# A new order table for all engines of a recurrence and gating kernel, and the shift of a normalisation made only where it is read

## The chip, the cores and the metric

The kernel runs on one core of a Trainium2 chip. A core has a matrix engine (TensorE, PE in the profile), a vector engine (VectorE, DVE), a scalar engine (ScalarE, ACT), a general engine (GpSimd, POOL) and a sync engine (SyncE, SP) that here only issues transfers. Each works through its own queue of instructions in order, and semaphores hold an instruction back until what it needs is there. The metric is device time in microseconds (us) of one execution. Of the kernel before, three executions gave a median of 138.45 us (138.4 to 139.81).

## The reference

Two stages follow each other. The first is a gated linear recurrence over 4 batches, 8 heads, 768 steps, heads of 48; the second mixes its output over the sequence and gates it.

```
# stage 1, per batch and head
for t in range(768):
    state = alpha[t][:, None] * state + outer(k[t], v[t])      # 48 x 48
    y[t] = q[t] @ state
x = y with heads side by side                                    # 4 x 768 x 384
# stage 2
h = relu(x @ w_in);  u, v = h[..., :512], h[..., 512:]
v_n = (v - mean(v)) / sqrt(var(v) + 1e-6)                        # over the 512
v_s = w_spatial @ v_n + b_spatial                                # 768 x 768, over the sequence
out = (u * v_s) @ w_out                                          # 4 x 768 x 384
```

## The kernel before, in words

The sequence is cut into chunks of 128 steps, six to a batch, 24 in all. Inside a chunk the recurrence becomes matrix products: logarithms of alpha are summed by products with triangles of ones (`half`, `cum`, `cums`), exponentials of the sums scale k and q (`einv`, `eexp` on ScalarE; `kt`, `qt` as products), scaled k and q are transposed (`tr`, `trk`) and copied out of PSUM (`ev`, `evs`), their product is masked (`sc`, then `m` or `ms` on VectorE), and the masked product times v plus q times the old state gives y (`y`, `ya`), copied to SBUF as xT (`xe`). `upd`, `z`, `S`, `sb` carry the state from chunk to chunk; `vb` and `vp` bring v into place. The first four chunks are done together (`four_chunks`, pair numbers 0 and 1), chunks 4 and 5 as a pair (`pair`, number 2), chunks 6 to 9 together again (3 and 4), and the rest one by one (`single`).

Stage 2 works on tiles of 128 rows. `v` projects a tile to the 512 columns that are normalised, `ve` applies relu; `bn` (two VectorE instructions, lines 1068 and 1069) takes mean and variance; `rs` (ScalarE, lines 1078 and 1079) takes the reciprocal root for two tiles at once; `nm` (VectorE, line 1085, two instructions for a pair of tiles) writes shift = -mean * rstd; `vn` normalises a tile, on VectorE as (v - mean) * rstd (line 1097) or on ScalarE as v * rstd + shift (line 1093). Only ScalarE's form reads the shift. `u` and `ue` make the other half. `s` mixes over the sequence with the turned spatial weights (tiles 0 to 3 of a batch in a first part, tiles 4 and 5 in a second), `se` adds the bias on VectorE (line 1153), `g` multiplies by u (mostly GpSimd, line 190), `o` projects out, `oe` copies out of PSUM, `st` stores. The weights come as fp32 through two buffers, are cast to bf16 (`cast`), and the spatial ones are transposed on TensorE (`wt`, line 1018) and copied (`we`). A third load of weights needs the casts of the first to be done, a fourth those of the second, and so on.

Each of these is an entry of a list `ops`, made in the order of the program text, with the entries it depends on and the engines that may do it. The order in which all engines get their work is not computed in the kernel: it is written out in the string `PLAN` (lines 42 to 88). A word such as `P62@0:512#0` says: entry 62, on PE, its result in PSUM bank 0, and ahead of it a dummy product of 512 columns into bank 0. `D`, `A`, `G`, `S` stand for VectorE, ScalarE, GpSimd and SyncE. `replay` (line 110) goes through the words and emits each entry. As every engine works in order, the table fixes, for each engine, what it does and after what; waits between engines are put in from the data. The dummy products keep TensorE busy where the table expects it to have nothing to do.

Helpers hide some lines: copies are recorded at lines 179 and 181, relu at 185 and 187, products of two tensors at 190, and all accumulating matrix products of stage 2 at 1006.

Of the kernel before, what the change touches and what calls it, by code (L numbers as in the profile page):

```python
# [47 lines left out]
P123@7,3 P141@2 S20 G276 G277 G278 G17 G19 G18 D124 D125 P151@6 P187@7,4 P126@3 S23 S274 S273 D185 A152 A127 G186 G183
G113 G114 D182 P190@5,6 A189 A192 A142 P144@3 D137 P139@4 D188 D191 A140 G22 G21 D153 D143 P199@6,5 P196@2,7 P162@4
A280 A145 P287@0 A163 P154@1 P160@3 A279 A288 A155 D200 D201 D198 D197 D164 P193@4 A161 P156@7 A157 A165 D194 D146  # L50
P158@5 A159 G195 P202@1,2 P203 S26 A204 A147 D166 P290@4 P37@5,7 D38 P34@3,6 G24 S275 S384 S396 G25 S503 S29 D35
P207@1 D148 D208 D36 A39 A289 P205 P281@7 P40@3,5 A206 A282 A167 G10 D42 P210@2 D149 D150 D41 S385 S386 D168 D209 S398
S397 P284@5 P223@6 P219@3 P221@1 A211 A291 A224 A285 D212 A283 A220 A213 D295 D301 A286 A292 D214 D222 D215 A216
P225@6 P233@2 P217@3 P229@7 P237@0 A218 A28 D298 G297 G27 D304 G294 P226 D227 G300 G303 P43@3,5 D45 P230 P234 D231
D235 A293 A44 P46@4,6 P306@5,1 D308 P238 P49@7,3 D50 D51 A48 A47 A307 P309@2,6 P315@1,4 P312@5,7 P249@3 P250 A310 A316
A314 A296 A311 A299 D313 D317 D239 G236 D251 P338@4,1 P332@7,5 P245@0 P246 G302 G305 D333 D339 G232 P318@7,6,3,2 G240
G228 D340 D319 A507 G33 D334 D321 D247 P253@4 P330@7,1 P254 P241@5 P242 G320 A388 A400 A30 A337 A331 A32 G322 P389@0
D255 P345@7,6 D243 D324 D347 A390 P341@4 A391 P335@5 G31 G325 D394 D327 D346 G393 P401@3 A342 A336 A402 A403 P257@1
A392 S492 S387 A258 P259@4 P356@2 S399 G404 G248 G323 G326 S491 S557 P343@0,7 D405 P351@3,5 P407@1,6 A357 D328 A344
A350 A408 D353 D352 P359@2 G252 G395 P348@7 A349 P354@3 D409 S505 S494 S506 P418@6,1 P413@5,0 D358 S493 S504 S559 S547  # L60
S545 S608 S558 S548 S546 A355 A360 D415 D420 P508@7 P366@3 P410@0 P371@2 P377@1 D411 D414 A260 A509 P375@0 D419 A495
D361 A372 A561 P262@5 P496@6 G244 G329 G406 G256 A367 A376 A510 D368 G412 A497 A498 P416@0 P421@3 A422 G514 G502 G500
D378 D379 D513 G512 A417 P264@2 P267@4 A499 A362 A380 A268 D363 D501 P426@0 P423@1 P435@3 P437@6 D381 A365 A427 A424
P433@4 A434 A438 A382 D263 D436 P269@0 D364 D265 D425 D428 D383 P518@1 P369@4 A511 A270 P562@6 P373@2 A374 A429 A549
P439@7 A565 P526@0 D440 D519 P453@3 D430 D431 A432 A563 A564 D370 P449@7 P550@1 P515@2,5 A516 A551 A553 D517 A552 P454
D455 D527 D567 G566 G520 G554 G456 P441@4 P442 P445@5 D443 P450 D451 P465@6 P446 D555 D447 P530@7,4 P521@2,0 P569@1,3
D522 G448 G452 P469@5 P466 P457@2 P470 D523 D531 D532 G528 G444 D471 S620 A556 P572@7 D573 A570 P458 S622 S609 S560
A612 D467 D459 P613@4 P524@5 P533@1 A624 S610 A571 P576@7,3 P585@6,0 G574 A614 A525 D586 A615 A534 P625@5 A626 A568
G472 P535@2 A627 P461@1 S621 S611 S727 S715 S718 S623 S717 G617 D618 D578 D577 S730 S729 P473@6 G628 G575 P538@3
P581@7 A536 A616 A539 P462 S781 S716 A474 D629 P631@5,4 D587 A633 D463 D582 S728 A719 P588@3 S783 S769 S782 S770 S832  # L70
S771 A589 S784 S772 G619 G529 P579@1 A580 D632 D537 P634@7 P479@6 A630 A480 P720@5 G583 G468 D635 G636 A721 P642@3,4
P637@0,2 D540 G460 G584 P476@7 P601@6 P593@1 D643 D639 D638 A731 A723 D644 G726 G464 A602 A738 G724 P590@3 P597@6 A591
P732@0 D603 D592 A735 D477 P645@4 P640@3 A541 D542 D543 D594 A646 P485@2 A641 A785 A598 A486 D544 P650@4 P657@7 P742@6
A651 D743 D652 A733 A604 D605 D607 P488@3 P661@4 A658 A662 A734 P647@6 A489 A773 G736 P595@1 D648 D606 P482@4 D649
A483 A722 D744 P663@7 A664 D737 P599@6 P659@4 P786@3 A653 A600 P673@7 P669@0 P750@6 A596 A787 A788 P774@1 A775 A789
A776 S481 S844 S833 S834 A836 A780 S835 S845 A660 S846 D654 D655 D656 D751 D725 P674 P670 P677@6 P685@5 D671 P678
P665@0 D791 D752 D675 D779 G778 G792 D679 P796@7 P666 G790 D797 P686 G672 D687 D667 P739@6,4 P793@7,3 A848 A777 D794
P693@5 A740 A795 G680 G676 P805@0 P694 P849@7 P837@6 A838 A839 A850 A840 A851 D741 P745@3,4 P754@1,2 D695 G798 G668
D746 D806 D755 P689@5 P690 D691 D747 P681@3 P700@0 P682 P697@5 G843 D756 A698 D683 P703@4 D853 D842 D704 A701 P757@5
A758 P748@0 A749 A799 P800@6,7 D802 G841 G852 P809@3,2 P855@4,5 G807 G684 G696 G688 A856 G692 D810 P759@0 S847 P858@7  # L80
P762@3 D811 D801 P709@2 P812@6 A753 A760 P803@0 A857 D859 D761 D854 A813 A804 A763 P861@5,7 P866@4,1 S699 P712@6 D863
D868 D764 D867 D862 P825@7 A826 D827 P821@1 P817@3 P814@7 A818 A765 A815 A822 G860 P869@4 A870 S702 A713 S478 S266
S484 S490 S487 S705 S261 S475 S271 G808 P864@5 D816 P823@3 P819@1 D865 P874@4 D766 D768 A824 S714 A828 A820 A875 A767
A710 D829 P871@3 D830 D831 P887@5 P885@1 P881@4 D876 D872 D873 A877 D878 D879 P913@6 P706@2 A707 P893@3 P883@7 P897@0
A884 A886 A882 A888 P889@2 D880 P894 D895 G896 P890 P898 P905@5 P906 D891 D899 P901@2 P902 G900 P914 P909@0 P910
P917@3 D903 D892 D915 G916 D904 P926@6 P920@2 P918 S708 A927 S928 A921 S922 S711 D911 D907 D908 P923@6 G912 D919
P929@2 A930 D924 S925 S931 P935@3 D936 S937 P932@6 A933 S934 P938@3 D939 S940
"""

PAIRS = (2,)
QUADS = (0,3)
PLAIN = (0, 2)
IDLE = 16
STORE_TWO = (0, 2, 4)

# [1178 lines left out]
```

## Time and profile before

| | |
|---|---|
| median of three executions | 138.45 us |
| profiled execution | 139.19 us, of which the profile's span is 137.4 us |
| PE, DVE, ACT, POOL busy | 131.0, 120.8, 108.0, 87.2 us |
| read from memory, written | 23.60 MB, 4.72 MB |
| TensorE clock granted | 1.0 throughout |

The span runs from the first to the last instruction; some 1.8 us of the profiled execution lie around it. Busy time is a mean over the whole span, and the kernel has stages with different limits: it begins with loads (DMA queues are nearly full for the first 38 us, a mean of 313 GB/s), then the batches follow each other through all engines, and the last 14 us hold only the last batch's mixing, output projection and stores. In a row of the timeline the columns are start, length, engine, line, operation, output and inputs, shapes, count, and in brackets the engine's idle time before it with what ended it. A merged row with x2 or x4 holds instructions that follow each other; each is a little longer than its distance to the next, since the next one starts before the first has written out.

### The profile page before, as it was taken

The page shows a single profiled execution, that of the slowest core. Times are in us where ns is not written, and L with a number is a line of the kernel's source. Part 1 is how long each engine was busy: PE and PEld are TensorE (multiplying, and loading weights), DVE is VectorE, ACT ScalarE, POOL GpSimd, SP SyncE. Part 2 cuts the span into 40 slices and gives each one's busy share as a digit, 9 for nine tenths or more (in the row PEclk, how much of TensorE's full clock was granted, in tenths as well). Part 3 has the DMA queues.
Part 4 walks back from the last instruction along what each step waited for, and adds up shares of the span by engine and source line. Part 5 has one row for each costly group of instructions (what it writes and reads, how often), then busy time and mean ns, then how long its engine had stood idle before and what let it go on. Part 6 is the DMA issues. An engine that isn't in the chain of part 4 may idle for free.

```text
span 137.4 us, 5308 instructions
## 1 busy us (share of the span) xinstructions
PE 131.0 (95%) x2122; PEld 79.2 (58%) x2122; DVE 120.8 (88%) x300; ACT 108.0 (79%) x261; POOL 87.2 (63%) x146
## 2 busy tenths in 40 slices
PE   6899998999999999999999999999999999999990
PEld 3365554564646566566657666656566765565560
DVE  6259999979999999999899999997999999974871
ACT  3476998899989889999997989999965796954041
POOL 7365899967399789972079989620799842003560
PEclk9999999999999999999999999999999999999999
DMA  3999999599989796899999797899991497101055
GB/s 83 371 371 382 341 321 347 132 374 383 366 164 261 159 218 127 163 184 192 195 190 209 143 205 147 167 194 226 190 181 23 158 390 257 66 0 57 0 203 203
DMA packets 76473, 28.66 MB, mean 209 GB/s; under 512 B 63008, under 2 KB 74912, under 8 KB 76448
## 3 DMA queue, kind: packets, MB, share of 16 engines
q1 hardware_dynamic: 76416, 28.32, 78.6%
q8 instruction: 16, 0.26, 0.8%
q14 instruction: 9, 0.07, 0.2%
q0 software_dynamic: 32, 0.00, 0.0%
HBM read 23.60 MB, written 4.72 MB: 206 GB/s over the span
## 4 chain that ended last, share of the span: by engine, by line
PE 76%; ACT 6%; DVE 6%; DMA 5%; issue 3%; POOL 2%; SPq 0%; POOLq 0%; ACTq 0%
PE bank L1006 53%; DMA kc<-in_k_dram 5%; PE bank L961 3%; PE bank L945 3%; PE bank L989 3%; PE bank L417 2%; PE bank L855 2%; PE bank L899 2%; PE bank L837 2%; PE bank L933 2%; DVE vn L1097 1%; PE bank L795 1%; PE bank L772 1%; ACT uT L185 1%; DVE w_spT L181 1%
## 5 line engine op out<-in xcount | busy, mean ns | idle before, releaser
L1006 PE MATMUL bank<-w_spT,vn 128*128 128x384 bf16 x192 | 35.8, 327 | 0.3 <-DVE vn L1097 0.3
L190 POOL TENSOR_TENSOR gT<-vs,uT 128x384 bf16<-128x384 f32 x28 | 25.7, 933 | 14.3 <-DVE vs L1153 14.1
L190 POOL TENSOR_TENSOR kt<-kc,binv 128x384 bf16<-128x384 f32 x22 | 20.3, 931 | 20.3 <-ACT binv L909 15.2
L1006 PEld LDWEIGHTS <-vn 128*128 128x128 bf16 x192 | 17.4, 98 | 11.7 <-DVE vn L1097 0.7
L1006 PE MATMUL bank<-w_in,xT 128*128 128x512 bf16 x72 | 19.1, 380 | 0.2 <-ACT xT L179 0.2
L1006 PE MATMUL bank<-xT,w_in 128*128 128x384 bf16 x96 | 18.7, 326 | 0.0
L1006 PE MATMUL bank<-w_out_sb,gT 128*128 128x384 bf16 (+1 forms) x100 | 18.4, 320 | 0.0
L1153 DVE TENSOR_TENSOR vs<-bank,bsp_bc 128x384 f32<-128x384 f32 x31 | 16.3, 550 | 2.4 <-PE bank L1006 2.3
L950 DVE TENSOR_TENSOR ptm<-bank,mask 128x512 bf16<-128x512 f32 x28 | 17.9, 683 | 0.4 <-PE bank L945 0.2
L179 ACT COPY kqT<-bank 128x512 bf16<-128x512 bf16 (+1 forms) x20 | 15.0, 792 | 3.1 <-PE bank L989 1.9
L1068 DVE BATCH_NORM_STATS2 stats<-v_sb 128x6 f32<-128x512 bf16 x24 | 16.4, 682 | 0.2
L185 ACT ACTIVATE v_sb<-bank 128x512 bf16<-128x512 f32 x20 | 11.8, 599 | 1.8 <-PE bank L1006 1.5
L185 ACT ACTIVATE uT<-bank 128x384 bf16<-128x384 f32 x27 | 12.4, 495 | 0.7 <-PE bank L1006 0.6
L1006 PEld LDWEIGHTS <-w_in 128*128 128x128 bf16 x96 | 9.0, 98 | 6.7 <-DVE ptm L950 0.3
L190 DVE TENSOR_TENSOR qt<-qc,bank 128x384 bf16<-128x384 f32 x24 | 12.6, 545 | 0.2 <-DMA qc<-in_q_dram 0.2
L1006 PEld LDWEIGHTS <-gT 128*128 128x128 bf16 x100 | 9.3, 98 | 5.8
L179 ACT CAST xT<-bank 128x384 bf16<-128x384 f32 x23 | 10.4, 482 | 1.8 <-PE bank L417 1.4
L844 DVE TENSOR_TENSOR ptm<-bank,mask 128x512 bf16<-128x512 f32 x16 | 10.4, 684 | 0.0
L1006 PEld LDWEIGHTS <-xT 128*128 128x128 bf16 x72 | 6.2, 97 | 6.2 <-ACT xT L179 1.2
L179 ACT COPY raw_w<-bank 128x384 f32<-128x384 f32 x8 | 3.8, 480 | 7.3 <-PE bank L1006 7.2
L394 DVE TENSOR_TENSOR zs<-bank,state 128x384 f32<-128x384 f32 x16 | 8.8, 549 | 0.5 <-PE bank L933 0.4
L243 PE MATMUL bank<-junk 128*128 128x512 f32 (+3 forms) x14 | 8.0, 700 | 1.1 <-DVE junk L1242 1.1
(162 smaller groups left out, 265.4 us busy)
## 6 DMA issues: line engine op xcount, KB each, us to landing
ac<-in_alpha_dram SPq DMA_DIRECT2D x14, 192.0 KB, 4.4
kc<-in_k_dram SPq DMA_DIRECT2D x14, 192.0 KB, 4.0
qc<-in_q_dram SPq DMA_DIRECT2D x14, 192.0 KB, 4.4
vc<-in_v_dram SPq DMA_DIRECT2D x14, 192.0 KB, 4.1
raw_w<-in_moe_w_spatial_dram SPq DMA_DIRECT2D x3, 768.0 KB, 8.0
out_dram<-o_sb SPq DMA_DIRECT2D x9, 192.0 KB, 2.0
ac<-in_alpha_dram SPq DMA_DIRECT2D x2, 768.0 KB, 6.8
kc<-in_k_dram SPq DMA_DIRECT2D x2, 768.0 KB, 7.6
```

Of the source, the lines that this page charges most:

```text
L179: nc.scalar.copy(out=out, in_=in_)
L185: nc.scalar.activation(out=out, in_=in_, func=AF.Relu)
L190: ENG[eng].tensor_tensor(out=out, in0=in0, in1=in1, op=ALU.mult)
L243: nc.tensor.matmul(out=banks[n][:, 0:cols].rearrange("p (a b) -> p a b", a=4), lhsT=junk, rhs=junk[:, None, 0:cols // 4].to_broadcast([128 ...
L394: lambda _: nc.vector.tensor_tensor(out=zs[i % 3], in0=tp(), in1=state[(i - 1) % 3], op=ALU.add),
L844: nc.vector.tensor_tensor(out=ptm[n2][:, ci, s], in0=banks[sl.bank].rearrange("p (hp t) -> p hp t", hp=HP), in1=mask[:, 3][:, None, :].to_ ...
L945: nc.tensor.matmul(out=pt[s][:, hp, :], lhsT=kT[rows, hp, :], rhs=qT[rows, hp, :], start=True, stop=True)
L950: nc.vector.tensor_tensor(out=ptm[n2][:, ci, s], in0=banks[sl_p[s].bank].rearrange("p (hp t) -> p hp t", hp=HP), in1=mask[:, 2][:, None, : ...
L961: nc.tensor.matmul(out=place(to, 3 * hp + (0, 1, 1, 2)[x]), lhsT=heads(vb, hp, x), rhs=ptm[n2][:, ci, x // 2, hp, :], start=(turn == 0), s ...
L1006: nc.tensor.matmul(out=ps, lhsT=lhsT, rhs=rhs, start=first and n == 0, stop=last and n == len(pairs) - 1)
L1068: nc.vector.bn_stats(out=stats[tt % 2], in_=v_sb[n2][:, tt, :])
L1153: nc.vector.tensor_tensor(out=vs[d], in0=banks[sl.bank][:, 0:TH], in1=bsp_bc[:, th, :], op=ALU.add)
```

## The change

The table `PLAN` is replaced as a whole. It is a different order with different banks and dummy products, and part of the work is given to other engines: of 24 tiles 22 are normalised on VectorE and two on ScalarE (18 and six before); relu of u is on VectorE 9 times (5), copies of the turned spatial weights 4 times (8), copies of xT 4 times (1), of the output 4 times (7), casts of v 7 times (3). GpSimd does state products 16 times (14) and casts of the state 10 times (13). The loads begin alpha, v, k, q where they began alpha, k, v, q, and pair 2's alpha comes ahead of the first half of w_in, which was the other way round.

The list gets twelve more entries: `nm` is one entry for each tile, and emits its VectorE instruction only if the table normalises that tile on ScalarE. So that it can know this, `replay` first goes through the table and notes each entry's engine. A tile's `vn` then depends on its own `nm` alone. With the new table two of the 24 shift instructions are left.

```diff
 def replay(ops, held, warm, plan):
 
+    for word in plan.split():
+        op = ops[int(re.match("[A-Z]([0-9]+)", word).group(1))]
+        op.eng = LETTERS[word[0]]
     for word in plan.split():
         word, *junk = word.split(":")
...
-        def nm(_):
-            for x in (tt - 1, tt):
+        for x in (tt - 1, tt):
+            def nm(_, x=x):
+                if made[("vn", b, x)].eng == "DVE":
+                    return
                 nc.vector.tensor_scalar(
                     out=shift[n2][:, x:x + 1], in0=mvs[n2][:, x, 0:1], scalar1=rstd[n2][:, x:x + 1], scalar2=-1.0,
                     op0=ALU.mult, op1=ALU.mult)
 
-        op(("nm", b, tt - 1), "DVE", nm, [("rs", b, tt - 1), ("vn", b - 2, tt - 1), ("vn", b - 2, tt)])
-        for x in (tt - 1, tt):
+            op(("nm", b, x), "DVE", nm, [("rs", b, tt - 1), ("vn", b - 2, x)])
+
...
             op(("vn", b, x), "DVE ACT", vnf,
-               [("rs", b, tt - 1), ("nm", b, tt - 1)] + [("s", b - 2, d, th, 1) for d in range(NDS) for th in range(2)])
+               [("rs", b, tt - 1), ("nm", b, x)] + [("s", b - 2, d, th, 1) for d in range(NDS) for th in range(2)])
```

The first words of the two tables:

```diff
 PLAN = """
-D2 D0 D4 D1 G9 G11 G5 G6 D3 S56 S57 S59 S58 A60 S12 S169 S170 A61 S272 S171 D8 P62@0:512#0:512#0:512#0 P66@1 P67 P63
-P70@2 P71 P74@3 P75 A68 A64 D79 G82 P91@4,5 P52@6 A69 A72 A76 G7 A78 A92 A84 A65 G88 G87 A73 A77 D85 D90 D81 D93 D53
...
+S56 D2 G6 S59 D3 G9 S57 D0 D4 D1 G5 S58 G8 A60 S171 G11 A61 P70@0:512#0:512#0:376#0 G7 P74@1 P66@2 P71 D84 A87 P67 S12
+D81 P62@3 A68 D90 P63 A72 P128@4,5 A69 P75 D129 A64 D82 G85 S275 A78 D79 A76 A77 D88 S172 A135 A73 D83
...
```

More of the change, by code (lines that the diff above doesn't have):

```diff
@@ L48 @@
[L48 to L52, printed above, removed]
@@ L83 @@
[L83 to L87, printed above, removed]
+S56 D2 G6 S59 D3 G9 S57 D0 D4 D1 G5 S58 G8 A60 S171 G11 A61 P70@0:512#0:512#0:376#0 G7 P74@1 P66@2 P71 D84 A87 P67 S12
@@ new lines @@
+G185 P141@2 D137 G281 A111 S389 D112 P198@0,3 A145 P201@4,1 D200 P139@7 G113 A283 D202 P54@6 P195@3 G18 A142 D199
+P287@5 A140 G19 P290@4 D114 A288 P293@0 D196 G21 P163@7 A289 D203 A55 G197 P34@3,2 D143 A164 P204@1,6 A36 G17 D154
+P205 A294 P207 G22 S23 A206 P155@2 D146 A291 P159@1 S26 A208 P209@7 G306 D165 A295 S401 A156 P226@6 D301 A147 G10
+P161@2 A210 D160 D150 P157@5 D148 D149 A292 G303 D151 P224@7 A35 S392 D211 A158 P212@1 A166 D304 G24 P222@5 A227 D167
+D169 D213 A225 P284@3 G25 A162 S278 P37@6,4 D168 P40@7,1 A223 D38 P220@2 S391 A42 D39 D170 G27 A41 P315@5,6 D214
@@ new lines @@
+A774 D881 D826 A838 P715@5 D777 D775 D778 D841 D839 P885@4 D842 A840 D776 P899@3 A883 D886 P895@7 A722 D900 P901@4
+D716 P925@3 D884 S717 P917@5 S264 D887 S723 P905@2 S274 D896 A888 P909@0 D889 D891 D890 P718@7 D892 P897@6 A898 P910
+P906 D911 P902 P929@6 D907 D903 P913@2 D834 G904 P914 P926 D915 P918 G908 P893@1 D912 P921@2 G916 A894 D927 A719 P930
+D919 P922 S720 P932@7 G920 D923 P935@5 D928 A933 G924 D931 P938@2 S934 A936 P944@6 S937 A939 P950@5 S940 A945 P941@2
+D951 S946 P947@5 S952 A942 A948 S943 S949
```

68 lines of the change are left out of this document (34 added, 34 removed).

## The prediction

> **What bounds the kernel now.** I read the page first, then the windows, the waits of each engine, and the timeline around the last wait of TensorE (PE).
>
> ```profile
> PE 131.0 (95%) x2122; PEld 79.2 (58%) x2122; DVE 120.8 (88%) x300; ACT 108.0 (79%) x261; POOL 87.2 (63%) x146
> ```
>
> PE looks like the limit, but the share is a mean over two stages. The windows (PE, PEld, DVE, ACT, POOL busy, clock, DMA share, GB/s) part them:
>
> ```profile
> 0.00:38.50 38.50, 35.45 (x601) 19.50 (x601) 31.80 (x101) 30.84 (x71) 27.41 (x55) 1.00 0.97 313
> 38.50:134.20 95.70, 95.59 (x1521) 59.74 (x1521) 88.69 (x199) 77.04 (x191) 59.76 (x92) 1.00 0.74 167
> 134.20:137.40 3.20, 0.00 (x0) 0.00 (x0) 0.36 (x1) 0.16 (x1) 0.00 (x0) 1.00 0.54 192
> ```
>
> From 38.5 to 134.2 PE never rests, and a tail of 3.2 us follows. What can be won lies ahead of 38.5 us. The waits of PE from 38.5 on have one entry, and it is the end of the first stage:
>
> ```profile
> PE bank L1006 <- DVE vn L1097: 0.3, 1, 0.3
> ```
> ```profile
> 37.47 1.01 DVE L1097 TENSOR_SCALAR vn<-v_sb,mvs,rstd 128x512 bf16<-128x512 bf16 x1
> ...
> 37.51 0.82 POOL L181 CAST w_row<-raw_w 128x768 bf16<-128x768 f32 x1 [0.90 <-DMA raw_w<-in_moe_w_spatial_dram]
> ...
> 38.54 0.50 PE L1006 MATMUL bank<-w_spT,vn 128*128 128x384 bf16 x2 [0.29 <-DVE vn L1097]
> ```
>
> At 38.54 the first spatial product of tiles 4 and 5 (batch 0) waits for VectorE (DVE), which has just normalised tile 4. What holds DVE before that? Its own waits, 0 to 60 us:
>
> ```profile
> DVE kt L190 <- ACT binv L741: 3.6, 1, 3.6
> ...
> DVE w_spT L181 <- ACT rstd L1078: 0.7, 1, 0.7
> DVE kqT L181 <- ACT kqT L179: 0.3, 1, 0.3
> ```
>
> The first lies ahead of 8.4 us. After that DVE hardly waits for 50 us. So the head is bound by DVE, from its first qt product at 11.69 us (row below) on:
>
> ```profile
> 11.69:38.50 26.81, 25.33 (x543) 14.58 (x542) 25.54 (x60) 24.17 (x58) 20.32 (x33) 1.00 1.01 324
> 38.50:66.40 27.90, 27.86 (x548) 17.23 (x549) 27.12 (x61) 25.97 (x65) 21.44 (x30) 1.00 0.89 184
> 66.40:134.20 67.80, 67.72 (x978) 42.51 (x975) 61.57 (x138) 51.06 (x127) 38.32 (x62) 1.00 0.67 160
> ```
>
> DVE is busy 25.54 of 26.81 us and 27.12 of 27.90. Until 66.4 us both engines are full; only then DVE gets air. The change is judged by one question: when is DVE through with the tiles that PE waits for?
>
> **The change part by part.** *The shift.* Before, every pair of tiles has two small DVE instructions; only ScalarE's form of the normalisation reads their result.
>
> ```profile
> L1085 DVE TENSOR_SCALAR shift<-mvs,rstd x24: 182/206/216, 29.7 to 123.0; 128x1 f32<-128x1 f32 x24
> ```
> ```profile
> L1097 DVE TENSOR_SCALAR vn<-v_sb,mvs,rstd x18: 381/408/1010, 32.9 to 123.5; 128x512 bf16<-128x512 bf16 x18
> L1093 ACT ACTIVATE vn<-v_sb,shift,rstd x6: 806/815/840, 32.6 to 119.7; 128x512 bf16<-128x512 bf16 x6
> ```
>
> The new table puts two of the 24 tiles on ScalarE (six before), so 22 of 24 shifts vanish: half of a pair's 0.25 us (below) each, 2.75 us of DVE. It also moves four tiles to DVE, 1.28 us, and with them 3.3 us off ScalarE.
>
> *The order, first tight point.* Next I count what the table gives DVE from the first qt to the last normalised tile of batch 0. An instruction's pitch is its duration less about 0.08 us, by which the next one overlaps it, as the rows with several show:
>
> ```profile
> 9.88 0.81 DVE L181 CAST o_sb<-vc 128x384 bf16<-128x384 f32 x2
> ...
> 11.69 1.48 DVE L190 TENSOR_TENSOR qt<-qc,bank 128x384 bf16<-128x384 f32 x3 [0.20 <-DMA qc<-in_q_dram]
> 13.14 0.56 DVE L190 TENSOR_TENSOR state<-bank,bcq 128x384 f32<-128x384 f32 x1
> ...
> 14.54 1.08 DVE L181 COPY kqT<-bank 128x512 bf16<-128x512 bf16 x3
> ...
> 25.09 2.48 DVE L587 TENSOR_TENSOR ptm<-bank,mask 128x512 bf16<-128x512 f32 x4
> 27.49 0.69 DVE L1068 BATCH_NORM_STATS2 stats<-v_sb 128x6 f32<-128x512 bf16 x1
> 28.21 0.18 DVE L1069 BATCH_NORM_AGGREGATE mvs<-stats 128x2 f32<-128x6 f32 x1
> 28.31 0.54 DVE L394 TENSOR_TENSOR zs<-bank,state 128x384 f32<-128x384 f32 x1
> ...
> 30.68 0.62 DVE L181 COPY w_spT<-bank 128x384 bf16<-128x384 bf16 x2 [0.70 <-ACT rstd L1078]
> ...
> 31.55 0.69 DVE L187 TENSOR_SCALAR v_sb<-bank 128x512 bf16<-128x512 f32 x1
> ...
> 32.94 0.73 DVE L1097 TENSOR_SCALAR vn<-v_sb,mvs,rstd 128x512 bf16<-128x512 bf16 x2
> ...
> 36.76 0.33 DVE L1085 TENSOR_SCALAR shift<-mvs,rstd 128x1 f32<-128x1 f32 x2
> 37.01 0.55 DVE L187 TENSOR_SCALAR uT<-bank 128x384 bf16<-128x384 f32 x1
> ...
> 93.76 0.33 DVE L181 CAST sbd<-state 128x384 bf16<-128x384 f32 x1
> ```
>
> Both tables have 12 mask products (0.60), 6 statistics (0.82), 5 kqT copies (0.33), 4 zs (0.46), one v_sb, uT and state (0.61, 0.46, 0.47): 17.15 us. Before adds 8 qt (0.46), 5 w_spT copies (0.27), 4 tiles (0.32), 3 shift pairs (0.25): 7.06, in all 24.2. After adds 9 qt, 2 w_spT copies, 6 tiles, a v cast (0.36), an sbd cast (0.25): 7.2, in all 24.35. So the shifts' gain is spent again: the sum is the same. The same PE work lies ahead of the point (25.7 us by my count of products).
>
> What differs is start and stops. Before took 26.79 us (11.69 to 38.48) for 24.2: 0.7 of the excess is the wait for rstd, 0.6 the long tile at 37.47, some 0.2 two small waits, 1.1 scattered gaps. In the new table 1.7 us of other DVE work (a statistic, qt, uT) stand between the statistics and the tile that needs rstd, and 2.8 us for the next pair, so this wait should go.
>
> The start: v is now loaded ahead of k.
>
> ```profile
> 5.35 1.58 ACT L683 ACTIVATE la<-ac 128x768 bf16<-128x768 f32 x2 [3.33 <-DMA ac<-in_alpha_dram]
> ...
> 8.40 1.55 DVE L190 TENSOR_TENSOR kt<-kc,binv 128x384 bf16<-128x384 f32 x2 [3.59 <-ACT binv L741]
> ```
> ```profile
> 1.21 6.25 DMA kc<-in_k_dram
> ```
>
> Four loads of one size end at 5.35, 7.46 and, for the last, 11.69 us: 2.1 us each, so the third, now k, lands near 9.6 instead of 7.46. Three kt products on DVE follow (two before, 1.55 us): 2.0 to 2.4 us, to 11.6 to 12.0. The qt, which need q at 11.69, then start at 11.7 to 12.0; I take 11.9. What hides the late k is v's casts, done meanwhile.
>
> On SP's queue half a load (1.05 us) of pair 2's alpha also passes the first w_in.
>
> ```profile
> 13.65 0.62 POOL L181 CAST w_in<-raw_w 128x512 bf16<-128x512 f32 x1 [1.37 <-DMA raw_w<-in_moe_w_in_dram]
> ```
>
> w_in lands near 14.7 instead of 13.65. POOL's new order puts a state product and an sbd cast ahead of the w_in casts, which end near 16, so this costs nothing; without them it would cost POOL that 1 us. The last four stores are the same four in another order.
>
> So the last tile ends at 11.9 + 24.35 + 1.1 = 37.35 if no tile is held up, 1.1 us ahead of before.
>
> *The tiles against GpSimd (POOL).* This speaks against the change. The tile of 37.47 took 1.01 instead of 0.41 us, and a POOL cast ran from 37.51 to 38.33. In the new table tiles 2 to 5 of batch 0 all go through DVE, at a time when POOL has three w_sp casts (0.82) and two kt (0.91) to do, 4.3 us within some 5. A tile that started under a running POOL product was not always held:
>
> ```profile
> 91.00 0.91 POOL L190 TENSOR_TENSOR kt<-kc,binv 128x384 bf16<-128x384 f32 x1 [2.98 <-ACT binv L909]
> ...
> 91.70 0.41 DVE L1097 TENSOR_SCALAR vn<-v_sb,mvs,rstd 128x512 bf16<-128x512 bf16 x1
> ```
>
> Bounds: nothing, and four times 0.6 = 2.4 us. I take one and a half such holds, 0.9 us, nearer to the row at 37.47 than to none, as POOL is so full. That gives 38.25, a gain of 0.25.
>
> The Trainium skill, page "SBUF — State Buffer", section "Who interferes with whom", says that a copy, cast or tensor_scalar of DVE in a two-port mode and a GpSimd instruction exclude each other, and that whichever issues first keeps the port pair for its whole length. By that rule each tile issued under a POOL cast waits to its end. The row at 37.47 agrees, the one at 91.70 does not show it.
>
> *Second tight point.* From there to the first product of batch 1 DVE has 25.8 us by the same pitches (26.8 before, which took 27.8, to 66.3). With the same excess of 1.0: 26.8. PE's own work in between is 25.7 by its pitches, 26.7 at the pace of before (26.8 by pitches took 27.85). DVE and PE come out level again, no slack, no gain: 65.05. Behind it PE has 67.7 by pitches, 69.0 at the pace of before (66.5 took 67.8): 134.05.
>
> *Rest.* PE's work is unchanged, the dummy products ahead of the first spatial product are 2592 columns instead of 3040, which stand in idle time. Across all engines DVE's sum stays at 118, ScalarE loses 5 us, POOL none. The last output piece goes to ScalarE behind a whole one at a 0.37 pitch: under 0.1 us more in the tail. Sum: 134.05 + 3.2 = 137.25 against 137.4, 0.2 less. The profiled execution took 139.19 us, 1.8 outside its span, the median is 138.45: I carry the difference over to the median, 138.2.
>
> **The rivals.**
> *Faster.* All tiles fall between POOL's instructions, qt starts at 11.7, and DVE, no longer stopped by rstd, has half the scattered gaps: 0.9 + 0.2 + 0.5 on top of 0.25, so 136.6. For it: tiles of batches 1 to 3 ran free of holds before. Against: the second tight point must give way too.
>
> *Slower: the port.* Tiles 2 to 5 of batch 0 each held 0.6 (2.4, 1.5 over my term), and one or two of batch 1, where no slack is left (0.6 to 1.2): 140.6. It decides from a fourth hold on. The page named above would make this the rule.
>
> *Slower: w_sp late.*
>
> ```profile
> 23.31 1.73 POOL L181 CAST w_in<-raw_w 128x512 bf16<-128x512 f32 x3
> ...
> 25.07 0.37 SPq L1048 DMA_DIRECT2D raw_w<-in_moe_w_spatial_dram  x1
> ...
> 31.39 1.59 POOL L181 CAST w_row<-raw_w 128x768 bf16<-128x768 f32 x2 [1.56 <-DMA raw_w<-in_moe_w_spatial_dram]
> ```
>
> The second w_sp load needs POOL's w_in casts. They ended at 25.04; the new table has some 13.4 us of POOL work ahead of the last one from about 14.9 on, so 28.3. With 6.3 us from issue to landing as here it lands at 34.6, its products come just in time for 38.25. Each us that POOL slips further is a us of the end; 1.5 late gives 139.9.
>
> *It doesn't do what it says.* The DVE sum shows this already: shifts go, tiles and casts come. It is part of the forecast.
>
> **How the numbers follow.** A measurement can tell about 1% (1.4 us) here. Forecast, within 1%, 138.2: 0.44. Faster: 0.23. The port: 0.19; w_sp and other waits of PE inside the full stage: 0.14. The forecast's own range is 137.1 (no hold) to 139.5 (a second 0.9 and a stop of 0.4). The whole range goes from a little under the faster case to the port's figure, 136.4 to 140.6; what is left out is the port's worse half and a part of the faster case, under 2 in 10.
>
> **What would show it.** Right: the rstd wait of DVE gone, vn 22 times on DVE with one or two over 0.8 us before 39, first qt at 11.7 to 12.0, the product of tiles 4 and 5 near 38.2, PE full behind it. Wrong: PE waits of over 0.5 us after 40 us, POOL waiting for w_sp past 35, or a first stage ended before 37.

## The result, and the profile after

The changed kernel takes 144.49 us (median of six, 143.88 to 145.57) where the kernel before takes 138.55 (median of six): 1.042 times as long, interval 1.0358 to 1.0481. Run once more on another chip it takes 143.54 against 138.45, 1.0386 (1.0344 to 1.0427). So it is slower by 5 to 6 us. Its profiled execution took 145.57 us with a span of 143.6, that of this other run, the second profile from here on, 143.11 with 141.2; before it was 139.19 with 137.4. Line numbers of the changed kernel lie four above those of before (six from line 1103 on).

The busy times of the page:

```profile
PE 131.8 (92%) x2120; PEld 78.8 (55%) x2120; DVE 123.6 (86%) x282; ACT 103.7 (72%) x253; POOL 88.8 (62%) x150
```

PE has 0.8 us more busy time than before, no more work; the span is 6.2 us longer. So the loss is waiting. The windows (length; PE, PEld, DVE, ACT, POOL busy; clock; DMA share; GB/s) say where. First the changed kernel, from PE's first product of the recurrence to its last, and the four stretches in which it rests:

```profile
28.00:38.50 10.50, 8.56 (x185) 5.17 (x186) 9.02 (x22) 8.09 (x23) 6.99 (x13) 1.00 0.94 286
...
50.00:57.00 7.00, 6.07 (x186) 3.93 (x186) 5.62 (x11) 5.82 (x14) 5.11 (x8) 1.00 0.98 242
...
65.00:74.00 9.00, 7.63 (x109) 4.73 (x108) 8.45 (x19) 7.25 (x23) 2.73 (x4) 1.00 0.92 180
...
105.00:128.00 23.00, 22.38 (x368) 13.64 (x367) 22.30 (x47) 17.16 (x39) 13.75 (x17) 1.00 0.15 53
...
6.74:140.07 133.33, 126.85 (x2114) 76.81 (x2113) 121.21 (x253) 101.17 (x250) 83.31 (x123) 1.00 0.77 199
```

The kernel before, whose PE ends 5.89 us earlier, so that its stretch from 99.11 on answers to the one from 105 on:

```profile
99.11:122.11 23.00, 22.95 (x410) 14.43 (x409) 22.39 (x49) 16.70 (x38) 12.59 (x16) 1.00 0.54 164
...
6.24:134.18 127.94, 126.37 (x2116) 77.37 (x2115) 117.32 (x264) 105.68 (x259) 83.47 (x129) 1.00 0.81 209
28.00:134.18 106.18, 105.79 (x1694) 65.45 (x1692) 98.19 (x227) 87.22 (x218) 65.99 (x103) 1.00 0.77 186
```

And the changed kernel in its second profile:

```profile
28.00:38.50 10.50, 9.51 (x191) 5.75 (x192) 9.50 (x23) 8.94 (x27) 8.16 (x13) 1.00 1.03 312
...
50.00:57.00 7.00, 7.00 (x173) 4.30 (x160) 7.00 (x14) 6.62 (x16) 5.20 (x8) 1.00 1.01 198
...
63.00:72.00 9.00, 7.68 (x112) 4.76 (x110) 8.10 (x18) 7.26 (x23) 2.67 (x4) 1.00 0.96 188
...
6.97:137.64 130.67, 126.19 (x2114) 76.34 (x2113) 120.87 (x253) 101.30 (x250) 82.94 (x123) 1.00 0.79 203
...
102.50:125.50 23.00, 22.38 (x367) 13.65 (x366) 22.31 (x47) 17.22 (x39) 13.80 (x17) 1.00 0.19 70
```

Between its first and last product PE rests 6.48 us (133.33 - 126.85), 1.57 before, 4.48 in the second profile. PE's last end comes 5.89 us later than before: 4.91 of rest, 0.50 of a later start (6.74 for 6.24), 0.48 of busy time. In the second profile it comes 3.46 later: 2.91 of rest, 0.73 of start, 0.18 less busy time. From 28 us on before rests 0.39. The changed kernel rests 1.94, 0.93, 1.37 and 0.62 in the four stretches, in the second profile 0.99, 0, 1.32 and 0.62 in the stretches that answer to them. So the third and the fourth are lasting, the first varies, and the second was that one execution's. What ended PE's waits (engine, line <- what it waited for: total, times, longest):

```profile
PE bank L1022 <- POOL w_row L185: 1.3, 1, 1.3
...
PE bank L937 <- ACT uT L189: 0.9, 1, 0.9
PE bank L421 <- POOL state L194: 0.8, 1, 0.8
PE bank L1010 <- DVE v_sb L191: 0.8, 2, 0.4
```

The second profile has the second of these with 1.1 and the fourth with 0.6, and not the third. Its page has a wait of 1.3 at line 1022 too, but it is another one: it stands ahead of the transposition of the first load of spatial weights, where the first profile waits 1.03 as well, up to 28.39. For the second load, which the last twelve of the 24 below read, PE does not wait there:

```profile
28.79 0.35 PE L1022 MATMUL bank<-ident,w_row 64*128 64x64 bf16 x12 [1.27 <-POOL w_row L185]
...
35.63 0.75 PE L1022 MATMUL bank<-ident,w_row 64*128 64x64 bf16 x24
```

**The first stretch** reads along the timeline of the changed kernel's first profile, from GpSimd through TensorE and ScalarE to VectorE:

```profile
35.19 0.91 POOL L194 TENSOR_TENSOR kt<-kc,binv 128x384 bf16<-128x384 f32 x1
36.05 1.74 POOL L185 CAST w_row<-raw_w 128x768 bf16<-128x768 f32 x2
...
36.99 0.35 PE L1022 MATMUL bank<-ident,w_row 64*128 64x64 bf16 x12 [1.25 <-POOL w_row L185]
...
37.38 0.86 ACT L183 COPY w_spT<-bank 128x384 bf16<-128x384 bf16 x2 [1.14 <-PE bank L1022]
...
38.51 0.37 ACT L730 ACTIVATE bcq<-bank 64x16 f32<-64x16 f32 x2
...
35.28 0.96 DVE L1103 TENSOR_SCALAR vn<-v_sb,mvs,rstd 128x512 bf16<-128x512 bf16 x1
...
36.70 0.40 DVE L1103 TENSOR_SCALAR vn<-v_sb,mvs,rstd 128x512 bf16<-128x512 bf16 x1
...
38.91 0.56 DVE L194 TENSOR_TENSOR qt<-qc,bank 128x384 bf16<-128x384 f32 x1 [0.99 <-ACT bcq L730]
39.47 0.74 DVE L1103 TENSOR_SCALAR vn<-v_sb,mvs,rstd 128x512 bf16<-128x512 bf16 x2
...
38.38 3.10 PE L1010 MATMUL bank<-w_spT,vn 128*128 128x384 bf16 x18
```

The second load of spatial weights landed at 35.71, while GpSimd was at a `kt`. GpSimd casts them from 36.05, PE waits 1.25 us to transpose them, ScalarE 1.14 to copy what PE transposed. Only behind these copies does it make the factors `bcq` for which VectorE waits 0.99 with a `qt`; behind that `qt` stand the tiles 4 and 5. The thirteenth of the 18 products, the first that reads them, starts at 40.33 (38.38 + 12 x 0.163). In the second profile GpSimd begins these casts at 35.15, VectorE does not wait for `bcq`, and the product starts at 39.38.

**The third stretch**, ScalarE, VectorE and PE of the changed kernel:

```profile
69.90 0.50 ACT L915 ACTIVATE bank<-bank 128x384 f32<-128x384 f32 x1
71.72 0.36 ACT L920 ACTIVATE bc<-bank 64x4 f32<-64x4 f32 x2 [1.32 <-DVE qt L194]
72.09 0.49 ACT L189 ACTIVATE uT<-bank 128x384 bf16<-128x384 f32 x1
...
71.14 1.00 DVE L194 TENSOR_TENSOR qt<-qc,bank 128x384 bf16<-128x384 f32 x2
...
72.63 0.33 PE L937 MATMUL bank<-vb,kt 128*128 128x96 bf16 x4 [0.93 <-ACT uT L189]
```

ScalarE is free from 70.40 on but waits 1.32 us until the `qt` of VectorE has read the same PSUM bank. Its next instruction is the relu that frees the bank PE wants for chunk 12's state update, and PE waits 0.93. In the table the words stand as `D562 A560`: the `qt` of chunk 14 one word ahead of `ebc`, the exponential of its totals. Both only read; the one whose word comes later waits for the other. Before, `ebc` stood 19 words ahead.

### The profile page after: what moved, and what is told of

It reads as the page before. It is cut to its first block, busy times and chain, and to the rows that moved or that the text cites. A ratio compares the mean times of both kernels' runs of the same rounds, so it can differ in the third digit from the quotient of the medians.

```text
span 143.6 us, 5265 instructions
## 1 busy us (share of the span) xinstructions
PE 131.8 (92%) x2120; PEld 78.8 (55%) x2120; DVE 123.6 (86%) x282; ACT 103.7 (72%) x253; POOL 88.8 (62%) x150
## 4 chain that ended last, share of the span: by engine, by line
PE 40%; DVE 28%; DMA 16%; ACT 7%; issue 3%; POOL 3%; ACTq 0%; DVEq 0%; SPq 0%; POOLq 0%
PE bank L1010 27%; DMA kc<-in_k_dram 9%; DMA ac<-in_alpha_dram 7%; DVE ptm L954 5%; DVE stats L1072 4%; DVE qt L194 2%; DVE ptm L848 2%; DVE zs L398 2%; DVE vn L1103 2%; PE bank L993 2%; PE bank L949 2%; PE bank L722 2%; PE bank L965 2%; DVE kt L194 2%; DVE kqT L185 1%
## 5 line engine op out<-in xcount | busy, mean ns | idle before, releaser
L194 POOL TENSOR_TENSOR gT<-vs,uT 128x384 bf16<-128x384 f32 x28 | 26.7, 964 | 21.4 <-DVE vs L1159 21.2
L1010 PE MATMUL bank<-w_spT,vn 128*128 128x384 bf16 x192 | 34.9, 326 | 0.6 <-DVE v_sb L191 0.4
L194 POOL TENSOR_TENSOR kt<-kc,binv 128x384 bf16<-128x384 f32 x21 | 19.4, 933 | 14.9 <-ACT binv L913 6.4
L1010 PE MATMUL bank<-xT,w_in 128*128 128x384 bf16 x96 | 19.4, 326 | 0.0
L189 ACT ACTIVATE uT<-bank 128x384 bf16<-128x384 f32 x23 | 10.9, 495 | 6.1 <-PE bank L1010 6.1
L913 ACT ACTIVATE binv<-bank 128x384 bf16<-128x384 f32 x14 | 6.9, 494 | 6.4 <-PE bank L906 2.5
L183 ACT CAST xT<-bank 128x384 bf16<-128x384 f32 x20 | 9.1, 487 | 2.0 <-PE bank L421 1.9
L1103 DVE TENSOR_SCALAR vn<-v_sb,mvs,rstd 128x512 bf16<-128x512 bf16 x22 | 9.4, 463 | 0.7 <-ACT rstd L1083 0.7
```

Source lines behind the costliest of these rows:

```text
L183: nc.scalar.copy(out=out, in_=in_)
L189: nc.scalar.activation(out=out, in_=in_, func=AF.Relu)
L194: ENG[eng].tensor_tensor(out=out, in0=in0, in1=in1, op=ALU.mult)
L913: op(("einvs", i), "ACT", lambda _: nc.scalar.activation(out=buf, in_=sums(), func=AF.Exp, scale=-1.0), [("cums", i)] + readers("kt", j - ...
L1010: nc.tensor.matmul(out=ps, lhsT=lhsT, rhs=rhs, start=first and n == 0, stop=last and n == len(pairs) - 1)
L1103: nc.vector.tensor_scalar(out=vn[n2][:, x, :], in0=v_sb[n2][:, x, :], scalar1=mvs[n2][:, x, 0:1], scalar2=rstd[n2][:, x:x + 1], op0=ALU.su ...
```

## Experiments

**Which part of the change.** The shift alone: the table of before, its 24 normalised tiles on the same engines, only the 18 shifts that nobody reads left out:

```diff
-        def nm(_):
-            for x in (tt - 1, tt):
+        for x in (tt - 1, tt):
+            def nm(_, x=x):
+                if made[("vn", b, x)].eng == "DVE":
+                    return
```

And the table alone, the changed kernel with all 24 shifts:

```diff
-                if made[("vn", b, x)].eng == "DVE":
-                    return
```

> The order table of before on all five engines, and of the change only the per-tile shift that is skipped where VectorE normalises (18 of 24 tiles of this table). Theory A (the prediction's step): VectorE is relieved of some 18 x 0.125 = 2.2 us, of which 0.5 us lie ahead of the first s product; that product starts 0.3 us sooner at most and the rest lies beside a full TensorE, so 138.2 to 138.6 us. Rival: the head of the kernel is really set by VectorE, all 0.5 us and the later ones come through, 137.0 to 137.8 us. Either way the shift is no cause of the slowdown.

> The new order table with the shift computed for all 24 tiles, as before the change. Theory A (the new table alone makes the slowdown): VectorE gets 22 x 0.125 = 2.75 us back, the time is that of the changed kernel or up to 1.5 us above it, 144.5 to 146.0 us. Rival (skipping the shift has upset the tuned order): near 138.6 us.

Measured, both against 138.04: the shift alone 138.8, 1.0042 (1.0012 to 1.0072); the table alone 145.87, 1.0536 (1.0488 to 1.0583). The table makes the whole loss. The shift is worth nothing in the table of before; in the new one leaving it out saves about 1.2% (1.0536 against 1.042), and the last tile of batch 0 ends at 40.20 (39.25 in the second profile) instead of 41.17.

**Which stretch, by cutting the tables together.** The head of before up to the first spatial product, then the new table (`old_head`); and the new table up to the scores of chunk 8, then that of before (`new_head`). The first, against the changed kernel:

```diff
 PLAN = """
-S56 D2 G6 S59 D3 G9 S57 D0 D4 D1 G5 S58 G8 A60 S171 G11 A61
+D2 D0 D4 D1 G9 G11 G5 G6 D3 S56 S57 S59 S58 A60 S12 S171 S172
...
 P406@4 G299 P256@1 A395 D336 G243 A397
...
```

> All engines follow the table of before until the first s product of TensorE (38.5 us in the trace of before), and the new table from there on. TensorE reaches this place about 1.8 us late in the changed kernel (40.3 against 38.5 us). Theory A (two losses of their own, one of about 1.8 us ahead of this place and one of about 3 us between 50 and 74 us): 142.4 to 143.0 us, with TensorE's waits of 0.9 us near 54 us and 1.1 us near 71 us still there. Rival B (all later waits follow from the late loads of the head): 138.5 to 139.5 us and both waits gone. Rival C (what is lost in the head is caught up later anyhow): 144.5 us.

> The reverse: the new table until the score product of chunk 8 (50.7 us in the trace of the changed kernel), and the table of before from there on. Theory A: before's time plus the 2.4 to 2.6 us that TensorE has lost by there, 140.9 to 141.3 us, and no waits of TensorE above 0.5 us behind 51 us. Rival B (the loads are late when the old tail begins, and it waits for them as well): 143 to 145 us. Rival C (lost time is caught up): 138.6 us.

Measured: 146.3, 1.0562 (1.0518 to 1.0606), and 149.61, 1.08 (1.0749 to 1.0852). Both are worse than the change, because the seam itself makes waits, in the first a transposition whose PSUM bank the last `qt` ahead of the seam still holds:

```profile
37.52 0.41 PE L776 MATMUL bank<-ident,kt 64*128 64x64 bf16 x16 [2.71 <-DVE qt L194]
```

In the second PE waits 3.5 us for VectorE's `zs`. Neither says anything of the head. One thing holds: with the old head PE's wait ahead of chunk 12's state update is there again (1.1 us), so it belongs to the new table's own order there.

**One suspect at a time.** `ebc_first` puts the words of `ebc` of chunks 12, 14 and 15 ahead of the `qt` that read the same bank. No engine's own order changes, only who of the two waits:

```diff
-P262@4 D507 A505
+P262@4 A505 D507
...
-G573 D562 A560
+G573 A560 D562
...
-P448 A446 D574 G563 P452 A572 P524@4
+P448 A446 G563 P452 A572 D574 P524@4
```

> The changed kernel, with three words of the order table moved: the exponential of the chunk totals (ebc) of chunks 12, 14 and 15 stands ahead of the qt product that reads the same PSUM bank, not behind it. No engine's own order changes; only who waits for whom on that bank. Theory A (ScalarE's 1.3 us wait for VectorE's qt at 71.7 us holds the u eviction that frees the bank for upd of chunk 12, where TensorE waits 1.1 us at 72.6 us): that wait goes, 1.0 to 1.4 us below the changed kernel's 1.042 of before, so 1.032 to 1.035 of before. Rival (TensorE at this place is bound by VectorE, the wait moves to the next product): within 0.3% of the changed kernel.

Measured: 142.85 against 138.25, 1.0333 (1.0282 to 1.0385), which is 0.9% less than the change (1.2 us), or 0.5% (0.7 us) by the change's second measurement; its interval overlaps both of the change's. What the edit does to the rows is seen in `own_place` below, which has it too.

`w_sp_first` lets the second load of spatial weights pass the k load of chunks 6 to 9 and the alpha load behind it on SP, and its casts pass `kt` on GpSimd. `w_sp_and_ebc` adds the words of `ebc_first`.

```diff
-S276
...
-S389
...
-P293@0 D196 G21 P163@7 A289 D203 A55 G197
+P293@0 D196 P163@7 A289 D203 A55 D143 A164 G17 G21 G197
...
-S23 A206
+S23 S276 S389 A206
...
-G306
...
-G303
...
-P284@3 G25 A162
+P284@3 G25 G306 G303 A162
```

`w_sp_behind` is the counter-test in the kernel before, the same load put behind two others:

```diff
-S23 S274 S273 D185
+S274 S273 S23 D185
```

> The changed kernel, with the load of the second third of w_spatial ahead of the four-chunk k load on SyncE's queue, and on GpSimd the casts that free its buffer and that use it moved forward (the third w_in cast behind its two neighbours, the two casts of this load ahead of the two kt products of chunks 8 and 9). Theory A (the loads land in order, some 2.1 us each, so this one lands near 33.1 instead of 35.7 us and TensorE's transpose of its first tile no longer waits 1.4 us at 37 us): 0.8 to 1.4 us below the changed kernel, 1.032 to 1.037 of before. Rival (the k load now lands near 35.2 instead of 33.1 us and its kt products hold TensorE instead): within 0.3% of the changed kernel, or above.

> Both of these edits in one kernel. If the two losses are apart from each other (theory A of both), the gains add: 2.0 to 2.6 us below the changed kernel, 1.023 to 1.028 of before. Rival (what is gained in the head is lost at the next late producer): no more than the larger of the two.

> The kernel of before, its load of the second third of w_spatial moved behind the four-chunk q and k loads on SyncE's queue, as it stands in the changed kernel; nothing else. It would land 2.5 to 4 us later than 31.3 us. Theory A (the prediction's price: each microsecond of this load is a microsecond of the kernel, since TensorE's transpose at 32.3 us and all behind it follow): 140.5 to 142 us. Rival (the q and k loads land sooner by as much and TensorE has other work there): within 0.5 us of before.

Measured: 145.16, 1.0453 (1.0376 to 1.053); 143.72, 1.0373 (1.0302 to 1.0444); 139.88, 1.010 (1.0051 to 1.0149), all against 138.25. In `w_sp_first` the load landed at 33.28 instead of 35.71, PE does not wait for its transposition, and nothing is won: the spatial product now waits 0.58 for tile 5 on VectorE, which ends at 41.41. But this run does not single out the load. Its tiles 2 to 5 of batch 0 took 0.76 to 1.00 us each, some 1.8 us more together than at 0.41, beside GpSimd's casts and `kt`, and VectorE waited 1.16 us for a load of v at 23.31. GpSimd and VectorE:

```profile
33.33 1.66 POOL L185 CAST w_row<-raw_w 128x768 bf16<-128x768 f32 x2 [1.12 <-DMA raw_w<-in_moe_w_spatial_dram]
...
33.50 1.64 DVE L1103 TENSOR_SCALAR vn<-v_sb,mvs,rstd 128x512 bf16<-128x512 bf16 x2
...
39.74 1.67 DVE L1103 TENSOR_SCALAR vn<-v_sb,mvs,rstd 128x512 bf16<-128x512 bf16 x2 [0.16 <-ACT rstd L1083]
```

The load does cost when it comes late, about 1.4 us (1.010) for one put behind two others in the kernel before, where I had expected 2 to 4.

**The normalisation and the last batch.** `norm_only` moves the chain of statistics, root and tiles of batch 0 forward in the new table; `bank_swap` gives the first spatial product of the last batch another PSUM bank, since it waits for VectorE to free its own; `norm_early` and `all_fixes` put these on top of `w_sp_and_ebc`. Two of the moves of `norm_only`:

```diff
-P222@5 A227 D167 D169 D213 A225
+P222@5 A227 D213 D151 D211 A225
...
-S278 P37@6,4
+S278 A223 S391 D214 D304 D167 D169 P37@6,4
```

And `bank_swap`:

```diff
-P901@4
+P901@6
...
-P897@6
+P897@4
...
-P902 P929@6 D907 D903
+P902 D907 D903 P929@6
```

> The changed kernel with the normalisation chain of the head moved forward alone; loads, casts and ebc as in the changed kernel. Theory A (two chains, each hides the other): nothing is gained, since the transpose of w_spatial's third tile still waits for its load until 37 us, within 0.4% of the changed kernel (1.042). Rival (the normalisation on VectorE alone sets the end of the head, as the prediction had it for the kernel before): 0.8 us or more below the changed kernel, 1.036 or less.

> The kernel with both edits of w_spatial and ebc, and in its head the chain of the normalisation moved forward: TensorE's v product of tile 5 changes places (and banks) with a u product 1.9 us ahead of it, VectorE evicts it and takes its statistics behind tile 4's at once, ScalarE takes the third pair's rstd ahead of a u eviction; TensorE's transpose of the late k tile stands behind three s products. Theory A (the changed head has two late chains, the load of w_spatial and the last tiles' normalisation, and the one hides the gain of the other): the second half of the first s product starts near 39.1 instead of 40.0 us, 0.7 to 1.1 us less than with both edits (1.0373 of before), so 1.029 to 1.033. Rival (DMA landings alone set the head, whatever the order of VectorE): within 0.3% of 1.037.

> The changed kernel, of which only the PSUM banks of the first s product of batch 3 and of a u product behind it are exchanged. Theory A: the wait of 0.6 us at 125.8 us goes, and the time falls by 0.4 to 0.6 us, 1.038 to 1.039 of before. Rival: the wait moves on, 1.042.

> The same, and the first s product of batch 3 changes banks with a u product behind it, so that it no longer waits for VectorE's eviction of v tile 5 (0.6 us of TensorE at 125.8 us in the changed kernel). Theory A (each of these waits is a loss of its own): 0.5 to 0.7 us less than without it. Rival (the next products wait for the same tiles): no difference.

Measured against 138.47: 1.0444 (1.0388 to 1.0499), 1.0402 (1.0344 to 1.046), 1.0524 (1.0463 to 1.0585), 1.0483 (1.0435 to 1.0531). None gains. In `norm_only` and `norm_early` I had moved two `qt` back to make room, and PE then waits for the banks they hold; the row of `norm_only`:

```profile
36.80 0.51 PE L1022 MATMUL bank<-ident,w_row 64*128 64x64 bf16 x23 [1.19 <-DVE qt L194]
```

In `bank_swap` the wait of 0.45 moved down the order and grew to 1.00; the kernel is 1% slower by the medians, of which this explains less than half:

```profile
130.75 0.32 PE L1139 MATMUL bank<-b_sp_sb,ones_row 1*128 1x384 bf16 x1 [1.00 <-DVE vs L1159]
```

VectorE is nearly full in this stretch (22.30 of 23.00 us in the window above), so I take it that a bank freed for one product is taken from another. But it was as full before (22.39), where PE rested 0.05 us: its load alone does not make the rest of 0.62.

**Is it the tiles moved to VectorE?** `share_back` gives five of them, tiles 2 and 5 of batch 0 and 1, 2 and 5 of batch 1, back to ScalarE. `own_place` has the three words of `ebc_first` and makes the second load of spatial weights early, into two slots of v that are free at that time; `own_share` is both; `own_dve` is `own_place` with two tiles of batch 1 behind other VectorE work. `changed_again` is the changed kernel itself. Of `share_back`, two of the five moves:

```diff
-P37@6,4 D168
+S278 A168 A227 A225 A162 P37@6,4
...
-G561 A559 D438
+A438 A558 A444 G561 A559
```

`own_place`, beside the words of `ebc_first`:

```diff
+        if key == ("w_sp", 1):
+            w, before = io["vc"][:, 0:2].rearrange("p n f -> p (n f)").rearrange("p (n f) -> p n f", n=n), []
         op(key, "SP", lambda _: nc.sync.dma_start(out=w, in_=src), before)
...
+    made[("w_sp", 1)].deps += [made[("vb", j, par)] for j in range(2) for par in range(2)]
+    made[("vc", 3, 4)].deps += [made[("cast", "w_sp", 1, m)] for m in range(2)]
...
-S23 A206
+S23 S277 S276 S389 A206
...
-P284@3 G25 A162
+P284@3 G25 G10 G306 G303 A162
```

`own_dve`, against `own_place`:

```diff
-A505 D507 D369 P260@2 A568 S555 D429 A517
+A505 D507 P260@2 A568 S555 D429 D369 A517
...
-D437 D436 P569@2 A444 P455@5 D519 G561
+D437 P569@2 A444 P455@5 D519 D436 G561
```

> The changed kernel, with the five tiles of batches 0 and 1 that ScalarE normalised before (2 and 5 of batch 0; 1, 2 and 5 of batch 1) given back to it, each behind the rstd of its pair, with their five shifts on VectorE. Theory A (VectorE's larger share holds the head and the second stage; it sheds 4.0 us of normalisation and gets 5 x 0.2 us of shifts): 0.8 to 1.5 us below the changed kernel, 1.031 to 1.036 of before. Rival (TensorE waits for w_spatial and for banks that ScalarE frees, which now has 4 us more): 1.042 or above.

> The changed kernel with the ebc words moved (1.0333 of before by itself), and the second third of w_spatial loaded right behind the first into the two v slots that are free between 10 and 34 us, so that its issue waits for no cast; its casts follow those of the first third. It should land near 29.6 instead of 35.7 us, the k load near 35.2. Theory A (the load holds the head): TensorE's waits at w_spatial's transposes go but for the first, 1.0 to 1.4 us below ebc alone, 1.023 to 1.026. Rival (normalisation of tiles 4 and 5 and the late k tile are due at the same time): 1.030 to 1.034.

> own_place and share_back together. Theory A (two chains of the head end at the same time, the load's and VectorE's, and only both edits bring a gain): 1.2 to 2.0 us below ebc alone, 1.019 to 1.025 of before. Rival (the new table's head is late for a third reason, as the k load or the late products of TensorE): 1.030 or above.

> own_place (1.0333 of before), with VectorE's eviction of v tile 4 of batch 1 ahead of the normalisation of tile 1, and its qt of chunk 13 ahead of the normalisation of tile 4. Theory A (TensorE's waits of 0.3 us at 63.8 and 0.3 us at 67.3 us are VectorE's order of work): both go, 0.4 to 0.6 us, 1.029 to 1.031. Rival (VectorE is full there and the wait moves to the next product): 1.033.

> The changed kernel itself, unaltered, for a second profile and as a yardstick beside the next kernel. Theory A (the wait of 0.8 us at 56 us was one of that execution): no wait of TensorE above 0.6 us between 42 and 60 us, the waits at w_spatial's transposes and at upd of chunk 12 there again, 1.036 to 1.045 of before. Rival: the wait at 56 us is there again.

Measured: `share_back` 147.04, 1.0622 (1.0572 to 1.0672) and `own_share` 146.22, 1.0594 (1.0557 to 1.0631), both against 138.11. Giving tiles back makes it 2 to 2.6% worse. By the longest of `share_back`'s waits of PE, their place on ScalarE holds up the relu that frees PE's banks:

```profile
PE bank L1010 <- ACT uT L189: 1.6, 1, 1.6
```

So nothing is won by giving these five back, at these places; other places and the later batches were not tested. `own_place` takes 142.47, 1.0333 (1.0286 to 1.038). Its windows and its timeline, ScalarE and then PE:

```profile
28.00:38.50 10.50, 10.04 (x191) 5.81 (x192) 10.07 (x25) 9.67 (x28) 7.55 (x13) 1.00 1.00 308
...
63.00:72.00 9.00, 8.73 (x118) 5.49 (x117) 8.90 (x21) 7.95 (x23) 3.30 (x5) 1.00 0.97 192
...
6.59:136.83 130.24, 126.21 (x2102) 76.68 (x2113) 120.41 (x253) 101.34 (x250) 83.12 (x124) 1.00 0.78 204
28.00:136.83 108.83, 106.91 (x1686) 65.21 (x1694) 102.10 (x218) 82.78 (x209) 69.34 (x104) 1.00 0.74 180
```
```profile
67.49 0.50 ACT L915 ACTIVATE bank<-bank 128x384 f32<-128x384 f32 x1
67.90 0.35 ACT L920 ACTIVATE bc<-bank 64x4 f32<-64x4 f32 x2
68.28 0.49 ACT L189 ACTIVATE uT<-bank 128x384 bf16<-128x384 f32 x1
...
69.23 0.33 PE L937 MATMUL bank<-vb,kt 128*128 128x96 bf16 x4
```

ScalarE goes straight on, PE doesn't wait, and the nine us from 63 on hold 0.27 of rest where they held 1.37 and 1.32. That is what the order of two readers of a bank cost. The early load (landed at 30.56) shows no gain: from 28 to 38.5 PE rests 0.46 instead of 0.99 to 1.94, but ahead of 28 us it rests 2.11 (4.03 in all, less 1.92 from 28 on) where the second profile of the change has 1.5. Up to 38.5 that is 2.57 against 2.47, and the time is that of `ebc_first`, which lacks the early load. Ahead of 28 us VectorE waits 0.38 for q and 0.56 for v. Both loads were issued before the early one (at 12.46 and 15.10, that at 21.61), in the order of the changed kernel, so why they came late is open. `own_dve` takes 142.54 against 138.45, 1.028 (1.0236 to 1.0324), the best of the mended tables, and its interval overlaps those of `own_place` and `ebc_first`. No table with the new order came near the kernel before.

## Why the prediction was wrong

I forecast 138.2, with 136.4 to 140.6 as the range; it is 144.5, and slower was the case I gave 0.33. The sum had four terms behind each other. Here is each with the two profiled executions, from these rows of the changed kernel and of its second profile:

```profile
68.66 3.04 PE L1010 MATMUL bank<-w_spT,vn 128*128 128x384 bf16 x16
```
```profile
37.42 3.10 PE L1010 MATMUL bank<-w_spT,vn 128*128 128x384 bf16 x18
...
66.14 2.99 PE L1010 MATMUL bank<-w_spT,vn 128*128 128x384 bf16 x16
```

| term (us) | predicted | profiled | second profile |
|---|---|---|---|
| to the product of tiles 4 and 5 | 38.25 | 40.33 | 39.38 |
| from there to batch 1's first product | 26.8 | 28.33 | 26.76 |
| from there to PE's last end | 69.0 | 71.41 | 71.50 |
| tail, and what lies outside the span | 3.2 + 1.8 | 3.53 + 1.97 | 3.56 + 1.91 |
| sum | 139.05 | 145.57 | 143.11 |

**"Behind it PE has 67.7 by pitches, 69.0 at the pace of before" is the step that failed most, and in both executions alike: 2.4 to 2.5 us.** The sum of an engine cannot see who waits for whom: PE rests 1.70 and 1.78 us in this term. I carried the pace of a stretch without a wait over to a table whose words I had counted and not followed. 1.1 us of it are the two readers of one bank at 70 us (1.37 and 1.32 of rest, 0.27 with the words exchanged), and `ebc_first`, which mends nothing else, is 0.7 to 1.2 us faster by the medians. 0.6 us are rest in the last batch, where PE waits for VectorE to free a bank; what in the order makes that wait is open. The other 0.7 is no rest: PE is busy 69.7 us in this term in both executions, where the forecast had 69.0. VectorE, whose sum over the kernel I had unchanged (its busy time is 123.6 for 120.8) and to which I had given air here, is busy 65.1 of 71.4 us, 61.6 of 67.9 before; that these 3.5 us more hold PE is not shown.

**The first term, "the product near 38.2", missed by 1.1 to 2.1 us.** The sum of VectorE was right as far as it went: two shifts left of 24, 22 tiles. But the first `qt` came at 12.25, and at 12.55 in the second profile (11.7 to 12.0 forecast; the three `kt` began at 10.12 and 10.41, where I had k landing near 9.6), and the wait for rstd is still 0.55 and 0.54 where it should have gone. From there to the last tile VectorE took 27.95 and 26.70 us, for my 24.35 of work, 1.1 of gaps and 0.9 of holds, 26.35 in all. The second profile:

```profile
12.55:39.25 26.70, 24.23 (x565) 14.75 (x562) 25.50 (x57) 24.26 (x61) 20.05 (x30) 1.00 1.01 321
```

Here "the head is bound by DVE" holds: VectorE is busy 25.50 of 26.70 us, and of the miss of 1.13 the late start makes 0.65. In the first profile it is what failed: VectorE also waits 0.99 for ScalarE, which waits for PE, which waits for the weights. I had this as the rival with the late w_sp: 34.6 for the landing, 35.71 in the profile. The sign that I named, GpSimd still waiting for these weights past 35, is not there: GpSimd was at a `kt` when they landed and went straight on to them. What the load costs by itself stays open, since `w_sp_first` is mixed with the held tiles and `own_place` with the late q and v.

**The second term was right** in the second profile, to within 0.1. In the first profile it has 1.5 more: PE stood 0.8 us ahead of an old-state product of chunk 9 and rested 0.93 in that window, at a place where the second profile has none. I put this down to the execution, not to the table; the like of it, 0.8 us at the same line, is in `own_dve` and missing in `own_place`. What causes it is open.

**The port** was my largest rival of the slower kind with 0.19, and in the changed kernel it is small. The 22 tiles:

```profile
L1103 DVE TENSOR_SCALAR vn<-v_sb,mvs,rstd 128x512 bf16<-128x512 bf16 x22 | 9.4, 463 | 0.7 <-ACT rstd L1083 0.7
```

Their mean is 0.463 us and their median 0.407, 1.2 us in all over the kernel. In the head one was held: the tile at 35.28 took 0.96, under GpSimd's `kt` of 35.19. The tile at 36.70 took 0.40 in the middle of GpSimd's two casts of 36.05 to 37.79. The rule of the Trainium skill, page "SBUF — State Buffer", section "Who interferes with whom", that whichever of the two issues first keeps the ports, fits the first row and not the second. That it need not stay small, the four tiles of `w_sp_first` show, with 1.8 us.

**The shift.** The forecast had it that "the shifts' gain is spent again" by the tiles. The runs show something else: with no tile moved it is worth nothing in the table of before (138.8 against 138.04), and inside the new table it is worth 1.2%.

## What to carry to other kernels

When a hand-written order is replaced, sums of work by engine show whether it could be as fast, not whether it is: follow, for each place where two engines touch one PSUM bank or buffer, whose word comes first and what is queued behind the loser. Two readers that need nothing from each other can still be put in order by the program, and exchanging two words took 1.1 us of PE's rest away. A wait in a stage where three engines are nearly full should be mended only with an eye to what lies a microsecond behind it: of eleven mended orders here six were no faster than the change, two of them with that exchange. The three fastest all hold it, and only `own_dve` lies clear of the change's intervals. And one profile is not enough: the second profile of the same kernel had the long waits of the head at another place.

## What was unexpected of the hardware

A wait of PE in the middle of the kernel can cost twice, since the granted clock falls behind it. After the wait of 2.71 us in `old_head`, and behind 1.8 us of rest between 26 and 30 us in `share_back` (a wait of 1.60 up to 28.89), the windows say, `old_head` first:

```profile
38.00:42.00 4.00, 3.65 (x24) 1.93 (x24) 0.63 (x2) 2.37 (x5) 2.20 (x3) 0.65 0.84 155
```
```profile
26.00:30.00 4.00, 2.24 (x86) 1.31 (x84) 3.90 (x9) 2.68 (x7) 2.58 (x5) 1.00 1.09 361
30.00:32.00 2.00, 2.00 (x53) 1.08 (x30) 1.70 (x5) 1.67 (x5) 0.95 (x2) 0.61 0.91 187
...
66.00:70.00 4.00, 2.26 (x14) 1.22 (x13) 2.85 (x8) 3.90 (x11) 0.00 (x0) 1.00 0.93 183
70.00:72.00 2.00, 2.00 (x15) 1.11 (x15) 0.89 (x3) 1.69 (x5) 0.00 (x0) 1.00 0.99 197
```

The clock is 0.65 and 0.61 there (0.54 in the two us after that). In `table_alone` the same four us hold 1.4 of rest and the clock stays at 1.00, as it does behind every wait of 1.3 us or less in the changed kernel. Nor does every wait of 1.6 bring it down: the second one in `share_back` (1.64, up to 69.95), with as much rest in four us, leaves it at 1.00, so no threshold comes out of these runs. The Trainium skill, page "TensorE: Matmul & The Clock Gate", section "Why this matters for your kernels", asks for no idle gap of over about 3 us; here a wait of 1.6 was enough once, and the measured rows decide.
